# Attention backward: one block of E through GpSimd and the tile of G's products, and two more blocks of E turned by TensorE

## The chip, the cores and the metric

One Trainium2 chip, one of its cores. The core has five engines that run side by side and wait for each other by semaphores: TensorE (PE, with its weight loads as PEld), VectorE (DVE), ScalarE (ACT), GpSimd (POOL) and SyncE (SP, which here only issues DMAs). The metric is device time in microseconds; less is better. The kernel before takes 2192.32 us (median of 3 runs, 2185.16 to 2199.84).

## The reference

The kernel computes a transformer block and its gradients. With `x` of 2048 rows by 512, `xn = layernorm(x)`:

```python
out = x + attention(xn, wqkv, wo) * silu(mlp(layernorm(xn), w1, b1, w2, b2))
```

and the gradients of `out` against `x`, `wqkv`, `wo`, `w1`, `b1`, `w2` and `b2`. Attention has 32 heads of 16 columns each:

```python
scores = q @ k.T * Dh ** -0.5      # per head, 2048 x 2048
p = softmax(scores)
o = p @ v
```

Only attention's middle part concerns us. For each head and each tile of 128 keys by 512 queries the kernel forms E, the exponential of the scores, and G, which is E times (dO times V transposed). From E and G follow the output, the gradient of q (sums over keys) and, with E and G turned round so that queries lie on the partitions, the gradients of k and v (sums over queries).

## The kernel before

The work has three stages: a first one that prepares projections and hidden layers (until some 220 us), attention (220 to 1870 us), and the remaining gradients. The change lies in `attention_core`.

**Blocks and steps.** Attention runs over 64 blocks: 16 pairs of heads by 4 groups of 512 queries. A block has 16 steps, one per key block of 128 keys (`kb`). `g` counts the steps over all blocks, 1024 in all. The order of the work is written out by hand at the end of the function: one turn of the loop issues parts of several steps, so that the engines overlap. In the turn of step g, in program order:

- `emit_cO(g-2)`: a small DVE copy of one transposed 128x128 block from PSUM tile `tT` into `ek` (L1231), in some steps only.
- `emit_xt`, `emit_fin`: in steps 2 and 7, the end of the block before: a DVE copy (L1290), a reciprocal (L1310), and five small operations on GpSimd (L1311 to L1329), which also produce the weights W for Z.
- `emit_d(g)` and `emit_s(g+1)` on PE: two matmuls each, one per head of the pair. `s` has one PSUM buffer, `d` three.
- `emit_exp(g+1)`: ACT's exponential of `s` into `ets` (L1124).
- `emit_z(g-20)`: four matmuls on PE that sum up the gradients of k and v of the block before (L1350). Z is one PSUM buffer; eight units fill it (first the four for G, then the four for E), and DVE adds it to `acc` (L1364, or L1362 where it starts) in steps 3 and 11.
- `emit_x(g-1, ...)`: twelve matmuls on PE in three groups, for the sums over keys: two from E (L1248, L1251), one from G (L1255), which therefore waits for step g-1's products. The G group of step 0 is put off to step 2.
- `emit_T(g-1)`: PE turns blocks of E by matmul with the identity into `tT` (L1208, L1212), one PSUM buffer. In steps 1 and 6 `emit_XT` puts two more transposes, of float32, into the other half of `tT` (L1282).
- `emit_mult(g)`: two DVE products G = E x d, one per head, into `gts` (L1153). Between the two stand `xs`, a DVE copy in step 0 (L1264), and `acc`.
- In some steps a tick: a tiny GpSimd copy that reads `gts` (L1420) and holds back a load that GpSimd issues behind it.
- `emit_cT(g-1)`: ACT's copy of `tT` into `ek` (L1224).
- `emit_dmat(g)`: transposing DMAs that SP issues.

**How E and G are turned round.** A step's E has eight blocks of 128x128 (four query blocks, two heads), its G has eight too. G goes by DMA: after every second step one transposing DMA takes 16 blocks from `gts` (four buffers of two steps each) to `gk` (L1170). Of E's eight blocks PE turns seven, and the eighth goes by DMA from `ets` to `ekd` (L1180, L1184, L1186). `ets` is one tile of three slots of four steps each, used in turn, so that the exponential of step g writes where step g-12 stood. The eighth block is the last one (query block 3, second head) where `kb // 4` is even and the first one where it is odd, so that the two lie side by side in `ets` when two neighbouring slots are read; one DMA then takes eight blocks, every eight steps. Where the two slots are the last and the first of `ets`, there are two DMAs of four blocks.

**Which of the seven are put off.** In steps 1 and 6, where `tT` is shared, key blocks 0 and 5 have only four blocks turned at once (`cut` is 3). The other three of each go into later steps as an eighth transpose in `tT`, one per step, by the table `OLDER`: the key is the step whose transposes the block joins, the value is its key block and number. These are the blocks that the small DVE copy of `emit_cO` takes.

Of the kernel before, what the change touches and what calls it, by code (L numbers as in the profile page):

```python
# [1050 lines left out]
def attention_core(ctx, ctx_r, tc, k, grads, Oall, dQall, dKVT_out, ident_f32, ident_bf, npairs=16, nqc=4):  # L1051
# [12 lines left out]
    ekd = sb("ekd", 3)  # L1064
# [9 lines left out]
    ets = etp.tile([128, 3, 4, 2, 4, 128], bf16, name="ets")  # L1074
# [21 lines left out]
    def z_unit(g):  # L1096
        j = g // 16
        m = g % 8
        return (j, (g % 16) // 8, m % 4, m // 4) if 0 <= j < NB else None
# [4 lines left out]
    def emit_s(g, hj):  # L1104
        a = a_unit(g)
        if a is None:
            return
        j, kb = a
        op = op_of(j)
        qc = blocks[j][1]  # L1110
        r = 32 * hj
        if hj == 0:
            cur["s"] = ps_s.tile([128, 2, 512], f32, name="s")
        s = cur["s"]
        nc.tensor.matmul(s[:, hj, :], lhsT=op["KVT"][r:r + 32, kb * 128:(kb + 1) * 128], rhs=op["QDT"][r:r + 32, qc * 512:(qc + 1) * 512],  # L1115
                         start=True, stop=True, tile_position=(r, 0))
        st_et[g] = ets[:, g // 4 % 3]

    def emit_exp(g):

        a = a_unit(g)
        if a is None:
            return
        nc.scalar.activation(out=st_et[g][:, :, :, a[1] % 4, :].rearrange("k b h q -> k h b q"),  # L1124
                             in_=cur["s"][:].rearrange("k h (b q) -> k h b q", b=4), func=ACT.Exp)
# [15 lines left out]
    def emit_mult(g):  # L1141
        a = a_unit(g)
        if a is None:
            emit_xs(g - 1)
            emit_acc(g + ZOFF)
            return
        kb = a[1]
        if kb % 2 == 0:
            cur["gts"] = gtp.tile([128, 2, 2, 512], bf16, name="gts")
        gts = cur["gts"]  # L1150
        st_gt[g] = gts
        for hj in range(2):
            nc.vector.tensor_tensor(out=gts[:, kb % 2, hj, :].rearrange("k (b q) -> k b q", b=4),  # L1153
                                    in0=st_d.pop((g, hj))[:].rearrange("k (b q) -> k b q", b=4),
                                    in1=st_et[g][:, :, hj, kb % 4, :], op=ALU.mult)
            if hj == 0:
                emit_xs(g - 1)
                emit_acc(g + ZOFF)

    def emit_dmat(g):  # L1160
        a = a_unit(g)
        if a is None:
            return
        j, kb = a
        kc = kb // 4
        if kb % 4 == 1:
            blk[j]["Gk"][kc] = gbp.tile([128, 4, 2, 4, 128], bf16, name="gk")
        if kb % 2 == 1:
            gk = blk[j]["Gk"][kc][:, kb % 4 - 1:kb % 4 + 1]
            nc.sync.dma_start_transpose(out=gk.rearrange("q r h b k -> q (r h b) k"), in_=st_gt[g][:].rearrange("k a h q -> k (a h q)"))  # L1170


        sl = g // 4 % 3
        if kb % 8 == 4:
            ek = ekd.tile([128, 2, 4, 128], bf16, name="ekd")
            blk[j]["Ek"][(kc - 1, 3)] = ek[:, 0]
            blk[j]["Ek"][(kc, 3)] = ek[:, 1]
            blk[j]["ekd"] = ek
            if sl == 0:
                nc.sync.dma_start_transpose(out=ek[:, 0], in_=ets[:, 2, 3, 1].rearrange("k a q -> k (a q)"))  # L1180
        if kb % 8 == 6:
            ek = blk[j].pop("ekd")
            if sl == 0:
                nc.sync.dma_start_transpose(out=ek[:, 1], in_=ets[:, sl, 0, 0].rearrange("k a q -> k (a q)"))  # L1184
            else:
                nc.sync.dma_start_transpose(out=ek[:].rearrange("q c a k -> q (c a) k"),  # L1186
                                            in_=ets[:].rearrange("k s b h a q -> k (s b h) (a q)")[:, 8 * sl - 1:8 * sl + 1]
                                            .rearrange("k x q -> k (x q)"))
# [9 lines left out]
    def emit_T(g):  # L1198
# [7 lines left out]
        for i in range(cut(g), 7):  # L1206
            b = i + a[1] // 4 % 2
            nc.tensor.transpose(tb[:, i - cut(g), :], et[:, b // 2, b % 2, kk, :], ident_bf[:])  # L1208
        if older(g):
            kk2, i = older(g)  # L1210
            b = i + kk2 // 4 % 2
            nc.tensor.transpose(tb[:, 7, :], st_et[g // 16 * 16 + kk2][:, b // 2, b % 2, kk2 % 4, :], ident_bf[:])  # L1212
# [20 lines left out]
    def emit_x(g, part):  # L1233
# [9 lines left out]
        for c in range(4):  # L1243
            half, hj = c // 2, c % 2
            r = 32 * c
            ev = et[:, half::2, hj, kb % 4, :]
# [6 lines left out]
            else:  # L1253
                gv = st_gt[g][:, kb % 2, hj, :].rearrange("k (b q) -> k b q", b=4)[:, half::2, :]
# [77 lines left out]
    def emit_z(g):  # L1332
# [7 lines left out]
        for par in range(2):  # L1340
            kc = 2 * kp + par
            for hj in range(2):
                r = 64 * par + 32 * hj
                if part == 0:
                    mv = blk[j]["Gk"][kc][:, :, hj, qb, :]
# [4 lines left out]
                nc.tensor.matmul(Z[r:r + 32, :], lhsT=WT[j % 2][1 - part][:, qb, hj, :], rhs=mv,  # L1350
                                 start=(part == 0 and qb == 0), stop=(part == 1 and qb == 3), tile_position=(0, r))

    def emit_acc(g):
        u = z_unit(g)
        if u is None or u[2] != 3 or u[3] != 1:
            return
# [23 lines left out]
    for g in range(NSTEP - ZOFF):  # L1380
# [36 lines left out]
        for it in [x for x in late if x[0] <= g]:  # L1417
            late.remove(it)

            nc.gpsimd.tensor_copy(out=tick[:], in_=st_gt[g][0:1, kb % 2, 1, 510:512])  # L1420
# [123 lines left out]
```

## Time and profile before

| | |
|---|---|
| runs | 2192.32 us median, 2185.16 to 2199.84 |
| profiled execution | 2194.69 us, its span 2193.0 us, granted clock 0.995 |
| attention | some 220 to 1870 us of the span |
| PE, DVE, ACT, POOL busy, share of the span | 98%, 86%, 81%, 27% |
| exponentials (L1124) | 1024 of 1026 ns |
| ACT's copies of tT (L1224) | 898 of 532 ns (128x448), 126 of 372 ns (128x256) |
| products (L1153) | 2048 of 682 ns |
| small DVE copies (L1231) | 378 of 225 ns |
| transposes on PE (L1208, L1212) | 6790 and 378 |
| transposing DMAs gk<-gts | 512, 5.4 us from issue to landing (median) |
| transposing DMAs ekd<-ets | 171, 4.3 us from issue to landing (median) |

In a row of the profile stand the line of the kernel, the engine, the operation, the tile written and the tiles read, the shape, and the count; behind the bar the busy time in all, the mean duration of one in ns, and the idle time of the engine ahead of them with what ended it. Rows of a timeline start with the start in us from the span's beginning and the duration in us; several like instructions in a row are merged and counted (x3). Instructions of DVE, ACT and PE overlap at their ends: a product that takes 0.68 us lets the next one start after 0.60.

### The profile page before, as it was taken

The page shows a single profiled execution, that of the slowest core. Times are in us where ns is not written, and L with a number is a line of the kernel's source. Part 1 is how long each engine was busy: PE and PEld are TensorE (multiplying, and loading weights), DVE is VectorE, ACT ScalarE, POOL GpSimd, SP SyncE. Part 2 cuts the span into 40 slices and gives each one's busy share as a digit, 9 for nine tenths or more (in the row PEclk, how much of TensorE's full clock was granted, in tenths as well). Part 3 has the DMA queues.
Part 4 walks back from the last instruction along what each step waited for, and adds up shares of the span by engine and source line. Part 5 has one row for each costly group of instructions (what it writes and reads, how often), then busy time and mean ns, then how long its engine had stood idle before and what let it go on. Part 6 is the DMA issues. An engine that isn't in the chain of part 4 may idle for free.

```text
span 2193.0 us, 73789 instructions
## 1 busy us (share of the span) xinstructions
PE 2138.7 (98%) x30610; PEld 1173.8 (54%) x30659; DVE 1895.6 (86%) x3523; ACT 1782.5 (81%) x2481; POOL 596.8 (27%) x1373
## 2 busy tenths in 40 slices
PE   6999999999999999999999999999999999899999
PEld 3444555555555555555555555555555555444444
DVE  6677899999999999998999999999998998788647
ACT  5764899999999999998999999999998998675224
POOL 4275212232222222221313222222222222511003
PEclk9999999999999999999999999999999999999999
DMA  7786999999999999999999999999999999999975
GB/s 237 245 277 202 205 197 199 204 200 201 204 197 201 205 195 203 199 198 194 204 196 203 205 197 202 201 203 201 201 205 190 198 210 193 312 256 242 239 212 178
DMA packets 1422031, 461.11 MB, mean 210 GB/s; under 512 B 1334590, under 2 KB 1405886, under 8 KB 1421696
## 3 DMA queue, kind: packets, MB, share of 16 engines
q1 hardware_dynamic: 1407392, 425.46, 102.9%
q0 software_dynamic: 12720, 29.37, 5.1%
q8 instruction: 240, 3.93, 0.8%
q10 hardware_dynamic: 1584, 1.57, 0.2%
q14 instruction: 95, 0.78, 0.1%
HBM read 62.79 MB, written 64.75 MB: 58 GB/s over the span
## 4 chain that ended last, share of the span: by engine, by line
PE 89%; DMA 5%; DVE 3%; ACT 2%; issue 1%; SPq 1%; POOL 0%; DVEq 0%; ACTq 0%; POOLq 0%
PE tT L1208 21%; PE Z L1350 15%; PE d L1137 15%; PE X L1255 5%; PE X L1248 5%; PE X L1251 5%; PE s L1115 3%; DMA ekd<-ets 2%; PE ps_dy L909 2%; PE ps_dw L983 2%; PE ps_dw L742 2%; PE ps_h L352 2%; PE ps_m L367 2%; PE ps_dh L875 1%; PE ps_dxa L1027 1%; PE tT L1282 1%
## 5 line engine op out<-in xcount | busy, mean ns | idle before, releaser
L1153 DVE TENSOR_TENSOR gts<-d,ets 128x512 bf16<-128x512 f32 x2048 | 1302.1, 682 | 32.0 <-PE d L1137 13.7
L1124 ACT ACTIVATE ets<-s 128x1024 bf16<-128x1024 f32 x1024 | 1051.1, 1026 | 30.4 <-DMA ekd<-ets 10.3
L1224 ACT COPY ek<-tT 128x448 f32<-128x448 f32 (+1 forms) x1024 | 524.7, 512 | 114.9 <-PE tT L1208 33.2
L1208 PE MATMUL tT<-ident_bf,ets 128*128 128x128 bf16 x6790 | 558.4, 221 | 0.0
L1208 PEld LDWEIGHTS <-ets 128*128 128x128 bf16 x6790 | 382.8, 98 | 212.7 <-issue 199.7
L1137 PE MATMUL d<-QDT,KVT 32*128 32x512 bf16 x2048 | 478.4, 385 | 0.2 <-DVE gts L1153 0.2
L1115 PE MATMUL s<-QDT,KVT 32*128 32x512 bf16 x2048 | 401.9, 380 | 10.5 <-ACT ets L1124 10.4
L1248 PE MATMUL X<-ets,NAT 128*32 128x256 bf16 x4096 | 290.4, 273 | 0.0
L1251 PE MATMUL X<-ets,Lc 128*32 128x256 bf16 x4096 | 290.3, 273 | 0.0
L1255 PE MATMUL X<-gts,NAT 128*17 128x256 bf16 x4096 | 286.7, 273 | 0.0
L1350 PEld LDWEIGHTS <-W 128*32 128x32 bf16 x4096 | 105.7, 93 | 239.8 <-issue 236.9
L1420 POOL COPY tick<-gts 1x2 bf16<-1x2 bf16 x205 | 35.8, 174 | 728.6 <-DVE gts L1153 728.6
L1137 PEld LDWEIGHTS <-KVT 32*128 32x128 bf16 x2048 | 151.7, 90 | 114.5 <-issue 21.8
L1350 PE MATMUL Z<-gk,W 128*32 128x512 bf16 x2048 | 204.0, 390 | 1.4 <-DVE acc L1364 1.0
L1350 PE MATMUL Z<-ek,W 128*32 128x512 bf16 x1792 | 203.5, 389 | 0.0
L1251 PEld LDWEIGHTS <-Lc 128*32 128x32 bf16 x4096 | 109.9, 97 | 108.4 <-issue 0.5
L1231 DVE COPY ek<-tT 128x64 f32<-128x64 f32 x378 | 84.9, 225 | 90.9 <-ACT ek L1224 76.8
L1115 PEld LDWEIGHTS <-KVT 32*128 32x128 bf16 x2048 | 145.7, 91 | 25.5 <-issue 20.0
L1311 POOL TENSOR_TENSOR W<-NATQq,rL 128x128 bf16<-128x128 bf16 x64 | 25.5, 398 | 384.3 <-DVE rL L1310 328.7
L1255 PEld LDWEIGHTS <-NAT 128*17 128x17 bf16 x4096 | 112.9, 91 | 11.8 <-issue 3.1
L1248 PEld LDWEIGHTS <-NAT 128*32 128x32 bf16 x4096 | 109.5, 96 | 4.8 <-issue 4.7
L1350 PE MATMUL Z<-ekd,W 128*32 128x512 bf16 x256 | 99.6, 389 | 0.0
(252 smaller groups left out, 2467.2 us busy)
## 6 DMA issues: line engine op xcount, KB each, us to landing
gk<-gts SPq DMA_TRANSPOSE x512, 5.4
H1T_s<-h1r SPq DMA_DIRECT2D x28, 256.0 KB, 4.1
HGT_s<-hgT SPq DMA_DIRECT2D x8, 896.0 KB, 4.4
DH_s<-stg SPq DMA_DIRECT2D x12, 512.0 KB, 3.3
hch<-DH_s SPq DMA_DIRECT2D x12, 512.0 KB, 5.1
gp<-H1T_s SPq DMA_DIRECT2D x9, 512.0 KB, 7.1
out_dram<-ob_w POOLq DMA_DIRECT2D x36, 128.0 KB, 4.5
NAT_s<-NS SPq DMA_DIRECT2D x4, 1056.0 KB, 6.3
```

The source lines that it names most:

```text
L352: nc.tensor.matmul(ps[:], lhsT=w1_sb[:, ic, fc * 128:(fc + 1) * 128], rhs=yT[:, ic, g * 512:(g + 1) * 512], start=(ic == 0), stop=(ic == I ...
L1115: nc.tensor.matmul(s[:, hj, :], lhsT=op["KVT"][r:r + 32, kb * 128:(kb + 1) * 128], rhs=op["QDT"][r:r + 32, qc * 512:(qc + 1) * 512], start ...
L1124: nc.scalar.activation(out=st_et[g][:, :, :, a[1] % 4, :].rearrange("k b h q -> k h b q"), in_=cur["s"][:].rearrange("k h (b q) -> k h b q ...
L1137: nc.tensor.matmul(d[:], lhsT=op["KVT"][r:r + 32, kb * 128:(kb + 1) * 128], rhs=op["QDT"][r:r + 32, qc * 512:(qc + 1) * 512], start=True, ...
L1153: nc.vector.tensor_tensor(out=gts[:, kb % 2, hj, :].rearrange("k (b q) -> k b q", b=4), in0=st_d.pop((g, hj))[:].rearrange("k (b q) -> k b ...
L1208: nc.tensor.transpose(tb[:, i - cut(g), :], et[:, b // 2, b % 2, kk, :], ident_bf[:])
L1224: nc.scalar.copy(out=blk[j]["Ek"][kb // 4][:, kb % 4, c:7].rearrange("q i k -> q (i k)").bitcast(f32), in_=st_T[g][:, 0:(7 - c) * 64])
L1231: nc.vector.tensor_copy(out=blk[g // 16]["Ek"][kk // 4][:, kk % 4, i].bitcast(f32), in_=st_T[g][:, 448:512])
L1248: nc.tensor.matmul(X[r:r + 32, 0:256], lhsT=NATt[:, kb, hj, 1:33], rhs=ev, start=(kb == 0), stop=False, skip_group_check=True, tile_positi ...
L1251: nc.tensor.matmul(X[r:r + 32, 256:512], lhsT=Lc[:], rhs=ev, start=False, stop=False, skip_group_check=True, tile_position=(0, r))
L1255: nc.tensor.matmul(X[r:r + 17, 256:512], lhsT=NATt[:, kb, hj, 0:17], rhs=gv, start=False, stop=(kb == 15), skip_group_check=True, tile_pos ...
L1350: nc.tensor.matmul(Z[r:r + 32, :], lhsT=WT[j % 2][1 - part][:, qb, hj, :], rhs=mv, start=(part == 0 and qb == 0), stop=(part == 1 and qb = ...
```

## The change

Four things are altered together.

- E's eighth block no longer goes by a DMA of its own. In every step GpSimd copies it, 128x128, from `ets` into a ninth place of the `gts` tile, ahead of the products, and the DMA of `gts` takes 18 blocks in place of 16. `gk` has nine blocks per step, and Z reads the eighth block of E from there. `ekd` and its DMAs are gone.
- `ets` becomes 11 places of one step each, so that the exponential of step g writes where step g-11 stood, and a step's E lies together in memory. `gts` lists its blocks as eight and one.
- Key block 1 has only five blocks turned at once (`cut` is 2), and its other two join later steps: `OLDER` has eight entries in place of six. Before, the steps that take an older block are those with keys 4, 6, 7, 8, 12 and 13; after, 4, 6, 7, 8, 9, 10, 12 and 13.
- The four units of Z for E run from query block 3 down to 0, in place of 0 to 3, and `acc` follows the last one.

```diff
-    ekd = sb("ekd", 3)
...
-    ets = etp.tile([128, 3, 4, 2, 4, 128], bf16, name="ets")
+    NE = 11
+    ets = etp.tile([128, NE, 4, 2, 128], bf16, name="ets")
...
-        return (j, (g % 16) // 8, m % 4, m // 4) if 0 <= j < NB else None
+        return (j, (g % 16) // 8, m if m < 4 else 7 - m, m // 4) if 0 <= j < NB else None
...
-        st_et[g] = ets[:, g // 4 % 3]
+        st_et[g] = ets[:, g % NE]
...
-            cur["gts"] = gtp.tile([128, 2, 2, 512], bf16, name="gts")
+            cur["gts"] = gtp.tile([128, 2, 9, 128], bf16, name="gts")
...
+        b = 7 * (1 - kb // 4 % 2)
+        nc.gpsimd.tensor_copy(out=gts[:, kb % 2, 8, :], in_=st_et[g][:, b // 2, b % 2, :])
         for hj in range(2):
-            nc.vector.tensor_tensor(out=gts[:, kb % 2, hj, :].rearrange("k (b q) -> k b q", b=4),
+            nc.vector.tensor_tensor(out=gts[:, kb % 2, 4 * hj:4 * hj + 4, :],
...
-            blk[j]["Gk"][kc] = gbp.tile([128, 4, 2, 4, 128], bf16, name="gk")
+            blk[j]["Gk"][kc] = gbp.tile([128, 4, 9, 128], bf16, name="gk")
         if kb % 2 == 1:
             gk = blk[j]["Gk"][kc][:, kb % 4 - 1:kb % 4 + 1]
-            nc.sync.dma_start_transpose(out=gk.rearrange("q r h b k -> q (r h b) k"), in_=st_gt[g][:].rearrange("k a h q -> k (a h q)"))
...
-        sl = g // 4 % 3
-        if kb % 8 == 4:
-            ek = ekd.tile([128, 2, 4, 128], bf16, name="ekd")
...
-    OLDER = {4: (0, 0), 6: (0, 1), 7: (0, 2), 8: (5, 0), 12: (5, 1), 13: (5, 2)}
+            nc.sync.dma_start_transpose(out=gk.rearrange("q r x k -> q (r x) k"), in_=st_gt[g][:].rearrange("k a x q -> k (a x q)"))
+
+    OLDER = {4: (0, 0), 6: (0, 1), 7: (0, 2), 8: (1, 0), 9: (1, 1), 10: (5, 0), 12: (5, 1), 13: (5, 2)}
 
     def cut(g):
-        return 3 if g >= 16 and g % 16 in (0, 5) else 0
+        return {0: 3, 1: 2, 5: 3}.get(g % 16, 0) if g >= 16 else 0
...
                 elif 2 * qb + hj == 7 * (1 - par):
-                    mv = blk[j]["Ek"][(kc, 3)]
+                    mv = blk[j]["Gk"][kc][:, :, 8, :]
...
-        if u is None or u[2] != 3 or u[3] != 1:
+        if u is None or u[2] != 0 or u[3] != 1:
```

The other lines of the diff only follow the new shapes.

More of the change, by code (lines that the diff above doesn't have):

```diff
@@ L1207, in emit_T @@
             b = i + a[1] // 4 % 2
[L1208 removed]
+            nc.tensor.transpose(tb[:, i - cut(g), :], et[:, b // 2, b % 2, :], ident_bf[:])
         if older(g):
@@ L1245, in emit_x @@
             r = 32 * c
-            ev = et[:, half::2, hj, kb % 4, :]
+            ev = et[:, half::2, hj, :]
             if part == "e":
@@ L1350, in emit_z @@
                 nc.tensor.matmul(Z[r:r + 32, :], lhsT=WT[j % 2][1 - part][:, qb, hj, :], rhs=mv,
-                                 start=(part == 0 and qb == 0), stop=(part == 1 and qb == 3), tile_position=(0, r))
+                                 start=(part == 0 and qb == 0), stop=(part == 1 and qb == 0), tile_position=(0, r))
     def emit_acc(g):
         u = z_unit(g)
-        if u is None or u[2] != 3 or u[3] != 1:
+        if u is None or u[2] != 0 or u[3] != 1:
             return
@@ L1418, in attention_core @@
             late.remove(it)
-            nc.gpsimd.tensor_copy(out=tick[:], in_=st_gt[g][0:1, kb % 2, 1, 510:512])
+            nc.gpsimd.tensor_copy(out=tick[:], in_=st_gt[g][0:1, kb % 2, 7, 126:128])
             it[1]()
```

23 lines of the change are left out of this document (5 added, 18 removed).

## The prediction

> **What bounds the kernel now.** I read the page's first part, then the stage table, then one block of attention in the timeline. A "block" is 16 steps (one pair of heads, one fourth of the queries); a "step" is one key block. There are 64 blocks, and step n is the loop's turn with g mod 16 = n.
>
> ```profile
> PE 2138.7 (98%) x30610; PEld 1173.8 (54%) x30659; DVE 1895.6 (86%) x3523; ACT 1782.5 (81%) x2481; POOL 596.8 (27%) x1373
> ...
> 900.00:1200.00 300.00, 297.81 (x5102) 169.44 (x5102) 275.97 (x516) 272.92 (x375) 74.83 (x209) 0.99 1.19 199
> ```
>
> The second row is 300 us of attention: PE, DVE and ACT are busy for 298, 276 and 273 us. All three are nearly full, so any can set a step. Interval n is the time from exponential n's start to the next one's. A plain one takes 1.551 us, which is ACT's own sum (1.026 for the exponential, the rest for the copy of tT). Those behind an eighth transpose take 1.57 to 1.59. An undisturbed block takes 25.17 us (that of block 34, which begins at 1089.2).
>
> Stalls come on top, and the tile ekd shows the largest kind:
>
> ```profile
> L1186 SPq DMA_TRANSPOSE ekd<-ets x85: 1260/1270/2438, 234.0 to 1843.8; - x85
> ...
>   ACT ets L1124: 10.3, 11
> ```
>
> The second line is from "who waited for it": 11 exponentials sat idle for 10.3 us in all, until the transposing DMA had read the slot of ets that they write. One such place, PE's rows (the bracket is the idle time before) and the stretches around it (the column before the last two is the granted clock):
>
> ```profile
> 1029.79 0.38 PE L1137 MATMUL d<-QDT,KVT 32*128 32x512 bf16 x1
> 1031.97 0.39 PE L1115 MATMUL s<-QDT,KVT 32*128 32x512 bf16 x2 [1.80 <-ACT ets L1124]
> ...
> 1034.14 0.60 PE L1115 MATMUL s<-QDT,KVT 32*128 32x512 bf16 x2
> ```
> ```profile
> 1030.00:1032.00 2.00, 0.20 (x4) 0.02 (x2) 0.62 (x2) 1.10 (x2) 0.00 (x0) 1.00 0.98 218
> 1032.00:1034.00 2.00, 2.00 (x26) 1.14 (x25) 1.24 (x2) 1.37 (x2) 0.00 (x0) 0.64 1.19 269
> 1034.00:1036.00 2.00, 2.00 (x24) 0.69 (x23) 1.15 (x2) 1.56 (x2) 0.00 (x0) 0.51 1.10 234
> ```
>
> PE idles 1.80 us, and then its clock is 0.64 and 0.51 for 4 us. This stall costs 2.1 us at once and 1.4 after.
>
> **The change, part by part.**
>
> *1. The ekd transposes go: -15 us.* From block 1 on, the blocks exceed the undisturbed length by 22.9 us in total. Of that, 4.7 us recur with every change of the pair (0.23 us in its first block, 0.08 in its last) and stay. Of the 18.2 left, some 3 are single steps longer by 0.28 us at no fixed place; 15 stand in intervals 3 and 11, where exponentials 4 and 12 reuse the slot that SP's lagging ekd transfer still reads, and in the slow-clock steps behind them. Afterwards the slot of step g is written again at g+11, and its readers (PE, the products, GpSimd's copy) are then done for several us. Bounds: -18, and 0 if another late transfer takes the place.
>
> The clock is where a rule can be weighed. The row shows 1.80 us of idle followed by a clock of 0.64 and 0.51. The Trainium skill, "TensorE: Matmul & The Clock Gate" (section "Why this matters for your kernels"), asks for no idle gaps over about 3 us; by it no slow clock would follow here, and this part would be worth 12 rather than 15. The trace disagrees with it, and I go by the trace.
>
> *2. Key block 1 gives two blocks away: 0.* Step 2 carries the postponed products of key block 0 as well (eight X matmuls on L1255), and interval 3 behind it is 1.646 us. Two transposes fewer save 2 x 0.055 us there, and ACT's copy shrinks from 0.53 us towards the 0.37 of the 256-wide form. But the gain does not last: from step 0 to step 4 DVE runs without a gap (xs 0.68, two mults per step at a pitch of 0.60, xt 0.42, rL 0.20, acc 0.68). In block 34 the last X matmul of step 4 is already held until mult(3,1) ends (1097.39; the matmul starts at 1097.44, some 0.1 us late). PE coming 0.11 earlier waits 0.11 longer there. Bounds: -7 (63 x 0.11) and 0.
>
> *3. Two more small DVE copies, in steps 11 and 12: +22 us.* Before, the eighth transposes are issued in steps 5, 7, 8, 9, 13, 14, and the DVE copies two steps after their key block: 6, 8, 9, 10, 14, 15. After, steps 10 and 11 get an eighth transpose, and steps 11 and 12 a copy. Step 11 is one of the two that also add Z to acc. DVE in steps 10 to 12 of block 34:
>
> ```profile
> 1106.68 0.23 DVE L1231 COPY ek<-tT 128x64 f32<-128x64 f32 x1 [0.15 <-ACT ek L1224]
> 1106.82 1.89 DVE L1153 TENSOR_TENSOR gts<-d,ets 128x512 bf16<-128x512 f32 x3
> 1108.63 0.68 DVE L1364 TENSOR_TENSOR acc<-Z,acc 128x512 f32<-128x512 f32 x1
> 1109.23 1.88 DVE L1153 TENSOR_TENSOR gts<-d,ets 128x512 bf16<-128x512 f32 x3
> ```
> ```profile
> 1107.63 0.53 ACT L1224 COPY ek<-tT 128x448 f32<-128x448 f32 x1
> ...
> 1109.84 0.28 PE L1251 MATMUL X<-ets,Lc 128*32 128x256 bf16 x4
> 1109.95 0.30 PE L1255 MATMUL X<-gts,NAT 128*17 128x256 bf16 x4
> ```
>
> The small copy waits each time for ACT's copy of the same tT (bracket; all six kinds start 0.03 us behind ACT's end, and the next mult 0.17 behind it). In step 11 today, mult(11,0) starts at 1108.02, acc at 1108.63, mult(11,1) at 1109.23 and ends at 1109.91; the X matmul of step 12 that needs it starts at 1109.95, 0.11 behind the group before it, which is PE's own pitch. The slack is nil. After: the eighth transpose moves ACT's copy to about 1107.69, it ends at 1108.21, the small copy follows, and mult(11,0) starts at 1108.38: 0.36 late. acc, mult(11,1) and the X matmul follow, Z of step 12 waits for acc, the transposes of step 12 come 0.35 late, and so do s and the exponential of the next step, which today start as soon as ACT is free. 63 blocks x 0.35 = 22 us. Queued behind the added wait on DVE are mult(11,0), acc and mult(11,1); PE waits for the last. Nothing returns it: later steps are set by ACT at 1.551, and DVE is idle again (0.48) before step 14. Bounds: 63 x 0.14 (the copy's own pitch, without the wait) = 9, and 63 x 0.37 = 23. I take the long value because all six existing kinds show the wait. The two steps with eight transposes cost at most 63 x 2 x 0.02 = 3 beside it, and nothing where step 11's chain is longer.
>
> *4. 1024 copies on GpSimd: 0.* No row has a 128x128 copy there. The nearest:
>
> ```profile
> L1420 POOL COPY tick<-gts 1x2 bf16<-1x2 bf16 x205 | 35.8, 174 | 728.6 <-DVE gts L1153 728.6
> L223 POOL COPY NS<-nat 128x512 bf16<-128x512 bf16 x32 | 19.4, 633 | 43.3 <-ACT nat L215 42.1 <-DVE nat L217 1.1
> ```
>
> A straight line between the means (174 and 633 ns) gives 0.29 us for 128 elements; the ends are 0.17 and 0.63. 16 x 0.29 = 4.6 us per block on top of the 6.3 (75 of 300) leaves GpSimd under half busy. Each copy stands ahead of its step's tick and behind the five small operations of steps 2 and 7. Step 7 is the tight one: in block 34 these run from 1102.63 to 1104.62, behind a tick and a load, so copy(7) ends near 1104.9, while mult(7,1), which alone released the transfer, ended at 1103.44. The transfer thus gets ready 1.5 us later. Its tile of gts is wanted again by step 14 (its mult starts at 1113.1): 8.2 us later, against 5.4 us median and 8.6 at most from issue to landing. So it is covered, nearly always; without that cover each late microsecond would hold DVE, and PE behind it.
>
> *5. SP: 0.* Per eight steps it transposes 4 x 16 + 8 = 72 blocks of 128x128 today in five or six instructions, and 4 x 18 = 72 afterwards in four. An ekd issue takes 1.2 to 1.3 us of SP even for four blocks, a gk issue 1.6 at least (median 2.3, its wait counted), so SP is relieved; the rate per block is the open point (below). Z's second half runs in the other order with as many matmuls, and what it reads has landed some ten steps earlier.
>
> **Sum.** -15 + 0 + 22 + 0 + 0 = +7 us. The profiled execution took 2194.69 (span 2193.0 and 1.7 around it), so it would take 2202; the median of the runs shown is 2192.32, 2.4 lower, so the forecast is 2199. About 1% (22 us) is what a measurement of this kernel can tell from no change.
>
> **Rivals.**
>
> *The step-11 chain is shorter than I think.* If the new copies don't wait for ACT, or DVE finds slack for them, part 3 is at most 9, and part 2 may pay some of its 7: -15 - 3 + 4 = -14, so 2178 (2172 to 2188). For it: DVE is idle 0.15 us before step 10's copy and 0.48 before step 14's. Against: neither idle time lies between step 11's start and its acc.
>
> *The lag lives on.* The exponential no longer waits for ekd, but the 18-block transfer of a late step 7 or 15 does not free gts in time, and DVE stalls where ACT did; part 1 is then 0 and the sum +22: 2214 (2207 to 2222). For it: the largest landing time (8.6) is over the 8.2 that I count. Against: DVE waited only 0.6 us in all for gk transfers, though SP lagged then too.
>
> *The transposes bind (the slower side).* Place: SP's queue. In block 31 SP issued without a pause from 1010.45 to 1034.70: 140 blocks in 24.25 us, 5.77 per us; the kernel asks for 72 in 12.58, 5.72 per us. The point from which it decides is a rate 1% lower. If rows of 18 blocks go at 5.5, eight steps take 13.1 us, 0.5 more, 127 times: +64, about 2263 with the small terms. Against: the DMA packets are 256 bytes each whatever the row's length, and fewer instructions should raise the rate.
>
> *The port.* The small copies, xs and xt are DVE copies, and some will meet a GpSimd copy. If that locks them out for 0.29 us, the four or so per block with no slack behind them (steps 0 to 4, 11 and 12) would cost 63 x 4 x 0.29 = 73: 2272. In the rows, the 63 small copies that lie beside GpSimd's two-input operations take 225 ns, as the others do, and the 425 mults that do take 681, as the others do. The Trainium skill, "SBUF — State Buffer" (section "Who interferes with whom"), says that copies can enter a mode that takes a port pair shared with GpSimd, and that the loser is then held for the whole instruction. By that rule this rival would be the outcome; the trace does not bear it out for sources in PSUM, which all of these copies have.
>
> **How the numbers follow.** The forecast (2190 to 2206) gets 0.55, the shorter chain 0.21, the lag 0.12, the transposes 0.06, the port 0.03, and 0.03 is left for a faster surprise. The ends of the terms give -18 - 7 + 9 = -16 and 0 + 0 + 26 = +26, so 2176 to 2218 without the two dear rivals, which leaves out some 0.15; that is the range. Faster by over 1% (under 2170.4): 0.04. Slower by over 1% (over 2214.2): half of the lag's and both dear rivals, 0.14. Within 1%: 0.82.
>
> **What would show it.** Part 1: no exponential waits for a DMA, no stretch of attention with a clock under 0.9. Part 2: interval 3 falls from 1.65 to about 1.55, and interval 5 rises by as much. Part 3: interval 13 (exponential 13 to 14) grows from 1.55 to about 1.90, the X matmul of step 12 starts right behind mult(11,1), and step 11's small copy shows idle time behind ACT's copy. Part 4: GpSimd's copies at 0.29, mults still at 681 ns. Part 5: landing no later than about 6 us. The prediction is wrong if step 11's mult starts on time, if DVE waits for gk or GpSimd, or if mults get longer.

## The result and the profile after

The changed kernel took 2199.85 us (median of 22 runs, 2194.92 to 2217.09), the kernel before in the same comparison 2193.21 (22 runs, 2185.16 to 2203.54). The ratio is 1.0031, 95% interval 1.0017 to 1.0045. On another chip (the last experiment below) it was 1.0012, 0.9997 to 1.0026. So the change costs some 3 to 7 us; the first comparison tells this from nothing, the second does not. The forecast was 2199. The profiled execution took 2199.02 us, its span 2197.3.

The same two rows as before, the busy time of the whole span and 300 us of attention (PE, PEld, DVE, ACT, POOL, then granted clock, DMA share and GB/s):

```profile
PE 2149.0 (98%) x30659; PEld 1177.0 (54%) x30659; DVE 1916.6 (87%) x3649; ACT 1780.1 (81%) x2481; POOL 869.3 (40%) x2397
```
```profile
900.00:1200.00 300.00, 298.37 (x5108) 169.77 (x5109) 280.34 (x541) 272.79 (x376) 125.58 (x400) 1.00 1.13 200
```

DVE went from 276 to 280 us in this stretch, where it has its two more small copies per block, and GpSimd from 75 to 126. PE and ACT look as they did. What costs the time shows only in the lengths of single steps. These are the medians of the sixteen intervals over blocks 1 to 62, in ns, taken from the starts of the exponentials in each trace. In the last three columns stand the sum of the sixteen, then the 62 blocks together in us, and what of that lies above 62 undisturbed blocks:

```
interval     0    1    2    3    4    5    6    7    8    9   10   11   12   13   14   15 |   sum  62 blocks  above
before    1554 1551 1552 1646 1558 1644 1558 1574 1570 1573 1577 1558 1552 1554 1589 1562 | 25172  1583.6  22.9
after     1556 1551 1553 1552 1666 1647 1556 1575 1570 1575 1575 1576 1574 1880 1556 1594 | 25556  1587.7   3.3
```

Two large effects nearly cancel. The time above the undisturbed block fell from 22.9 us to 3.3, and the undisturbed block grew by 0.384 us, 23.8 us over 62 blocks. Most of the growth is interval 13 (+326 ns). The difference is +4.1 us, as the profiled executions have it (2199.02 against 2194.69).

Of the first effect, the exponentials' group shows what is gone. The columns behind the last bar are idle time before the instruction and what ended it; before, the first entry of this row was the DMA of `ekd`, with 10.3 of 30.4 us:

```profile
L1124 ACT ACTIVATE ets<-s 128x1024 bf16<-128x1024 f32 x1024 | 1051.6, 1027 | 16.7 <-PE d L1137 3.9 <-issue 1.4 <-POOL ndr L1299 0.2
```

The second effect is for the most part one place in each block. This is the changed kernel's timeline in steps 11 and 12 of block 34 (start, duration, engine, line; the bracket is idle time before). First DVE:

```profile
1108.93 1.29 DVE L1155 TENSOR_TENSOR gts<-d,ets 128x512 bf16<-128x512 f32 x2
1110.33 0.22 DVE L1215 COPY ek<-tT 128x64 f32<-128x64 f32 x1
1110.47 0.68 DVE L1155 TENSOR_TENSOR gts<-d,ets 128x512 bf16<-128x512 f32 x1
1111.07 0.68 DVE L1348 TENSOR_TENSOR acc<-Z,acc 128x512 f32<-128x512 f32 x1
1111.67 0.68 DVE L1155 TENSOR_TENSOR gts<-d,ets 128x512 bf16<-128x512 f32 x1
```

Then ACT and PE in the same window:

```profile
1109.77 0.53 ACT L1208 COPY ek<-tT 128x448 f32<-128x448 f32 x1
...
1111.81 0.40 PE L1334 MATMUL Z<-gk,W 128*32 128x512 bf16 x4
...
1112.24 0.45 PE L1239 MATMUL X<-gts,NAT 128*17 128x256 bf16 x4
...
1112.41 0.09 PEld L1239 LDWEIGHTS <-NAT 128*17 128x17 bf16 x2 [0.17 <-issue]
1112.62 0.56 PE L1192 MATMUL tT<-ident_bf,ets 128*128 128x128 bf16 x7
```

ACT's copy of tT ends at 1110.30, the added small copy starts 0.03 behind it, mult(11,0) at 1110.47, the addition to `acc` at 1111.07, mult(11,1) at 1111.67, ending at 1112.35. Four Z matmuls start at 1111.81, when the addition has read Z. The four X matmuls that read the products take 0.45, where the prediction's row of the same place has 0.30: the first starts at 1112.24 and the other three only at 1112.40, just behind mult(11,1). The transposes and the next s follow 0.3 late.

### The profile page after: what moved, and what is told of

Same layout as the page of the kernel before. It is cut to its first block, busy times and chain, and to the rows that moved or that the text cites. A ratio compares the mean times of both kernels' runs of the same rounds, so it can differ in the third digit from the quotient of the medians.

```text
span 2197.3 us, 74997 instructions
## 1 busy us (share of the span) xinstructions
PE 2149.0 (98%) x30659; PEld 1177.0 (54%) x30659; DVE 1916.6 (87%) x3649; ACT 1780.1 (81%) x2481; POOL 869.3 (40%) x2397
## 4 chain that ended last, share of the span: by engine, by line
PE 87%; DVE 6%; ACT 3%; DMA 2%; SPq 1%; issue 1%; POOL 0%; DVEq 0%; ACTq 0%; POOLq 0%
PE tT L1192 20%; PE Z L1334 15%; PE d L1137 14%; PE X L1239 6%; PE X L1232 5%; PE X L1235 5%; PE s L1115 3%; PE ps_dw L983 2%; PE ps_dy L909 2%; PE ps_h L352 2%; PE ps_dw L742 2%; PE ps_m L367 2%; DVE gts L1155 2%; ACT ek L1208 2%; PE ps_dh L875 1%; DVE acc L1348 1%
## 5 line engine op out<-in xcount | busy, mean ns | idle before, releaser
L1208 ACT COPY ek<-tT 128x448 f32<-128x448 f32 (+2 forms) x1024 | 518.4, 506 | 135.0 <-PE tT L1192 57.0
L1192 PE MATMUL tT<-ident_bf,ets 128*128 128x128 bf16 x6664 | 550.9, 221 | 0.0
L1192 PEld LDWEIGHTS <-ets 128*128 128x128 bf16 x6664 | 375.4, 98 | 210.5 <-issue 195.2
L1137 PE MATMUL d<-QDT,KVT 32*128 32x512 bf16 x2048 | 467.4, 384 | 0.0
L1153 POOL COPY gts<-ets 128x128 bf16<-128x128 bf16 x1024 | 280.3, 297 | 389.5 <-ACT ets L1124 388.1
L1334 PE MATMUL Z<-gk,W 128*32 128x512 bf16 x2304 | 302.9, 389 | 9.7 <-DVE acc L1348 1.1
L1239 PE MATMUL X<-gts,NAT 128*17 128x256 bf16 x4096 | 300.2, 273 | 0.0
L1137 PEld LDWEIGHTS <-KVT 32*128 32x128 bf16 x2048 | 145.9, 91 | 114.3 <-issue 21.5
L1215 DVE COPY ek<-tT 128x64 f32<-128x64 f32 x504 | 112.6, 223 | 97.1 <-ACT ek L1208 76.1
L1115 PEld LDWEIGHTS <-KVT 32*128 32x128 bf16 x2048 | 139.6, 91 | 12.2 <-issue 6.8
L1196 PE MATMUL tT<-ident_bf,ets 128*128 128x128 bf16 x504 | 110.4, 219 | 0.0
```

The costliest lines, as they stand in the source:

```text
L1137: nc.tensor.matmul(d[:], lhsT=op["KVT"][r:r + 32, kb * 128:(kb + 1) * 128], rhs=op["QDT"][r:r + 32, qc * 512:(qc + 1) * 512], start=True, ...
L1153: nc.gpsimd.tensor_copy(out=gts[:, kb % 2, 8, :], in_=st_et[g][:, b // 2, b % 2, :])
L1208: nc.scalar.copy(out=blk[j]["Ek"][kb // 4][:, kb % 4, c:7].rearrange("q i k -> q (i k)").bitcast(f32), in_=st_T[g][:, 0:(7 - c) * 64])
L1215: nc.vector.tensor_copy(out=blk[g // 16]["Ek"][kk // 4][:, kk % 4, i].bitcast(f32), in_=st_T[g][:, 448:512])
L1239: nc.tensor.matmul(X[r:r + 17, 256:512], lhsT=NATt[:, kb, hj, 0:17], rhs=gv, start=False, stop=(kb == 15), skip_group_check=True, tile_pos ...
```

## The experiments

Times of a run are compared with runs of the kernel before on the same chip; a ratio is to these, with its 95% interval.

### 1. Each half alone

The change without its second part:

```diff
-    OLDER = {4: (0, 0), 6: (0, 1), 7: (0, 2), 8: (1, 0), 9: (1, 1), 10: (5, 0), 12: (5, 1), 13: (5, 2)}
+    OLDER = {4: (0, 0), 6: (0, 1), 7: (0, 2), 8: (5, 0), 12: (5, 1), 13: (5, 2)}
...
-        return {0: 3, 1: 2, 5: 3}.get(g % 16, 0) if g >= 16 else 0
+        return 3 if g >= 16 and g % 16 in (0, 5) else 0
```

> The change without its second part: the GpSimd copy and the 18-block transposes stay, the blocks of E are given away in the steps of the kernel before (six of them, none of key block 1). Theory (the transposes of E by DMA cost 15 to 20 us, the two more small copies on DVE gave 22 to 24 back, the copies on GpSimd cost nothing): the excess over the undisturbed block falls from 22.9 us to about 3, the intervals 11 to 15 stand as before (1558, 1552, 1554, 1589, 1562 ns), so about 20 us under the kernel before, some 2174 us, ratio 0.991; by the prediction's own term of 15 us it would be 2177. Rival (the copies on GpSimd or the longer transposes have a price of their own, which the saved transposes covered): between 2185 and 2200 us, with multiplications longer than the 682 ns of before or stalls left on gk. Rival of the clock gate (12 us): 2181 us.

Measured: 2181.13 us against 2196.99, ratio 0.9926 (0.9915 to 0.9938), so -16 us. The 62 blocks take 1568.9 us, 14.8 less than before; the part above the undisturbed block is 5.2 (before 22.9), and the undisturbed block is 25.220 (25.172). The products take 683 ns. The theory holds in the main, nearer to the prediction's own 15 than to the 20 that I had made of it after the result. The 20 was missed twice over: the part above the undisturbed block did not fall to 3, and the undisturbed block did not stand as before. It is 0.048 us longer (intervals 4, 13 and 15 have 1574, 1588 and 1593 ns, interval 14 fell to 1557), 3.0 us over 62 blocks. So the GpSimd copies, the 18-block transposes and the new order show this price together; which of them it belongs to is not shown. The 2181 us of the rival with the clock was met only as a number: the kernel before stood at 2196.99 on this chip, and 12 us less would have been 2185. This version is faster than both kernels.

The second part alone, on the kernel before (the same two edits the other way round):

> The kernel before, with only the second part of the change: two blocks of E of key block 1 transposed in the steps of key blocks 8 and 9, and two of key block 5 moved to 10 and 12. The transposes of E by DMA stay, GpSimd copies nothing. Theory (the small copies in steps 11 and 12 alone make the loss): interval 13 goes from 1554 to about 1880 ns, 11 and 12 rise by some 20 each, the intervals 3 and 4 change places, so 22 to 24 us over the kernel before, about 2216 us, ratio 1.010 to 1.011. Rival (the loss needs the GpSimd copies beside it, or the tile of 18 blocks): less than 5 us over the kernel before, interval 13 below 1650 ns. Rival (the longer steps give the transposes of E by DMA time to land): 2200 to 2208 us, with interval 13 at 1880 and the stalls of 18 us at half.

Measured: 2208.63 us, ratio 1.0057 (1.0042 to 1.0073), +12.5 us (9 to 16). Interval 13 has the median 1876, 11 and 12 have 1575 and 1576, 3 fell to 1551 and 4 rose to 1641. So the undisturbed block grows as the theory says, by 0.355 us or 22 us in all, and needs neither the GpSimd copy nor the new tile for it. But the time rose by little more than half of that. The stalls were not halved, as the third reading had it: 21.3 us stand above the undisturbed block, before 22.9, and the wait for the DMA is all there.

```profile
L1124 ACT ACTIVATE ets<-s 128x1024 bf16<-128x1024 f32 x1024 | 1051.1, 1027 | 38.4 <-DMA ekd<-ets 13.4 <-PE d L1137 4.4 <-ACT ek L1224 2.9
```

A part of the answer stands in the single blocks. In 13 of 62, interval 13 is under 1700 ns, and these are blocks with a stall in interval 11 just ahead (1785 to 2816 ns), in which DVE has caught up before its copy is late. There the two losses are not added, which is worth some 13 x 0.3 = 4 us. But the profiled execution of this kernel was the longest of its six (2216.2), and its 62 blocks take 20.4 us more than those of before, with these 4 us already saved. What made the median 7.6 us shorter than this execution is in no trace and stays open. The halves measured alone add up to -4 us, the whole to +3 to +7, so they are not quite independent.

### 2. Which of the two added copies

Only the copy in step 11 is left (seven blocks given away, one of them of key block 1):

```diff
-... 8: (1, 0), 9: (1, 1), 10: (5, 0), 12: (5, 1), 13: (5, 2)}
+... 8: (1, 0), 9: (5, 0), 12: (5, 1), 13: (5, 2)}
...
-        return {0: 3, 1: 2, 5: 3}.get(g % 16, 0) if g >= 16 else 0
+        return {0: 3, 1: 1, 5: 3}.get(g % 16, 0) if g >= 16 else 0
```

> The changed kernel with seven blocks given away in place of eight: the step of key block 10 gets none, key block 1 gives one block away and not two. So of the two added small copies of DVE only that of step 11, beside the addition of Z, is left. Theory (this copy alone makes the loss): interval 13 stays near 1880 ns, above 1800 in any case, and the time near that of the changed kernel, 2196 to 2203 us. Rival (the loss is the sum of both copies, half each): interval 13 near 1720 ns, some 10 us less than the changed kernel, 2187 to 2192 us.

Only the copy in step 12 (the same, with `10: (5, 0)` in place of `9: (5, 0)`):

> The counterpart: seven blocks, the step of key block 9 gets none, so that of the two added small copies only that of step 12 is left. Theory (the copy in step 11 makes the loss): interval 13 falls to 1580 to 1650 ns (a copy in step 13 was worth 57 ns there), and the time to that of the change without its second part or up to 4 us more, 2181 to 2186 us on the chip of the first four runs, ratio 0.992 to 0.995. Rival (half each): interval 13 near 1720 ns, 2187 to 2192 us, ratio 0.996 to 0.998.

All transposes stay, but DVE's copy in step 11 is left out:

```diff
         kk, i = older(g)
+        if g % 16 == 9:
+            nc.gpsimd.memset(blk[g // 16]["Ek"][kk // 4][:, kk % 4, i], 0.0)
+            return
         nc.vector.tensor_copy(
```

> The changed kernel, all its transposes in place, without the small copy of DVE in step 11: the block is transposed into the tile tT but never read from there, GpSimd writes zeros in its place in the tile of E, so one block of key block 5 or 1 is zero in the output's sums (part of the computation is left out). Theory (the copy on DVE is the cost, not the eighth transpose on PE): interval 13 falls from 1878 to 1580 to 1650 ns, 14 to 18 us come back, 2182 to 2187 us. Rival (the eighth transpose on PE is the cost): interval 13 stays above 1800 ns, 2195 to 2203 us.

Measured on one chip (the kernel before 2193.04), with the medians of three intervals and the block:

```
                           time      ratio (95%)                interval 12   13   14    block
copy in step 11 only     2200.44   1.0024 (1.0005 to 1.0044)           1559 1897 1558    25568
copy in step 12 only     2182.66   0.9928 (0.9905 to 0.9951)           1594 1559 1594    25258
step 11's copy off DVE   2181.65   0.9928 (0.9904 to 0.9952)           1576 1571 1579    25251
```

All three fall as the theory has it, within a microsecond and some 20 ns of the bounds that it gave. The copy in step 11 alone makes the whole loss, the one in step 12 nothing that can be measured, and the eighth transpose on PE is not the cost, for it stays in the third kernel. DVE in the same steps of block 34 with only the copy in step 12:

```profile
1099.61 1.89 DVE L1155 TENSOR_TENSOR gts<-d,ets 128x512 bf16<-128x512 f32 x3
1101.41 0.68 DVE L1348 TENSOR_TENSOR acc<-Z,acc 128x512 f32<-128x512 f32 x1
1102.01 0.68 DVE L1155 TENSOR_TENSOR gts<-d,ets 128x512 bf16<-128x512 f32 x1
1102.61 0.21 DVE L1215 COPY ek<-tT 128x64 f32<-128x64 f32 x1
```

Exponential 12 starts at 1100.85 here and at 1110.20 in the changed kernel. Counted from there, the addition starts at 0.56 and mult(11,1) at 1.16; with the copy in step 11 it is 0.87 and 1.47. So the copy, 0.22 long, makes both late by 0.31, since it has to wait for ACT first. The second kernel also still gives one block of key block 1 away, and is no faster than the one that gives none (0.9928 and 0.9926): giving it away gains nothing that shows.

### 3. Other places for the copy

The eight blocks in other steps, none with its copy beside the addition:

```diff
-    OLDER = {4: (0, 0), 6: (0, 1), 7: (0, 2), 8: (1, 0), 9: (1, 1), 10: (5, 0), 12: (5, 1), 13: (5, 2)}
+    OLDER = {3: (0, 0), 4: (0, 1), 6: (0, 2), 7: (1, 0), 8: (1, 1), 11: (5, 0), 12: (5, 1), 13: (5, 2)}
```

> The changed kernel, with the same eight blocks given away in the steps of key blocks 3, 4, 6, 7, 8, 11, 12, 13 in place of 4, 6, 7, 8, 9, 10, 12, 13: the small copies of DVE stand in steps 5 and 13 in place of 11 and 12, none beside the addition of Z. Theory (the copy in the step of the addition is the price): interval 13 falls from 1878 to under 1600 ns, 18 us or more come back; the copy in step 5 stands behind the five steps in which DVE is late, and can cost up to its 0.29 us there (0 to 18 us over 62 blocks), so 2176 to 2194 us, the middle of which, 2182, is the likeliest. Rival (eight small copies on DVE cost this wherever they stand): 2197 to 2203 us, with the lost time in another interval.

Measured: 2186.02 us, ratio 0.9953 (0.9940 to 0.9965). Interval 13 has 1645, intervals 4 and 5 have 1670 and 1703, the block 25.336. So 0.22 of the 0.384 us came back. Interval 13 did not fall under 1600, as the theory had it. Against the kernel without the second part (25.220), the copy in step 5 costs 57 ns in the intervals 3 to 5 together, and the one in step 13 as much in interval 13. A small copy of DVE costs between nothing and 0.31 us here, by its step.

The copy of step 11 moved behind both multiplications:

```diff
-        emit_cO(g - 2)
+        if g % 16 != 11:
+            emit_cO(g - 2)
...
         emit_mult(g)
+        if g % 16 == 11:
+            emit_cO(g - 2)
```

> The changed kernel, with one operation moved: in step 11 the small copy of DVE stands behind both multiplications and the addition, not ahead of them. Theory (the copy ahead of them makes mult(11,0), the addition and mult(11,1) late, and the matmuls of G and Z in step 12 wait for these): interval 13 falls from 1878 to about 1600 ns, some 18 us come back, 2180 us. Rival (DVE has no slack for this copy anywhere between steps 11 and 13): the loss moves to interval 14 or stays, 2195 to 2203 us. Rival (the tile tT that is held longer stops the transposes of step 12): PE waits ahead of them for DVE, 2190 to 2205 us.

Measured: 2278.6 us, ratio 1.0378 (1.0364 to 1.0391), some 80 us slower than the changed kernel. The third reading named the mechanism and was far off in its price. There is one buffer for tT, so the transposes of step 11 wait until the small copy has read it. PE's rows in block 34:

```profile
1149.79 0.28 PE L1239 MATMUL X<-gts,NAT 128*17 128x256 bf16 x4
1151.55 0.55 PE L1192 MATMUL tT<-ident_bf,ets 128*128 128x128 bf16 x7 [1.47 <-DVE ek L1215]
```

PE stands for 1.47 us in each block (63 times, 92.8 us in all); interval 12 becomes 3102 ns, and interval 13 is back at 1557, because DVE catches up meanwhile. The run says that the copy cannot go there, and nothing on whether DVE has room for it.

### 4. What GpSimd's copies cost

The copy done twice:

```diff
-        nc.gpsimd.tensor_copy(out=gts[:, kb % 2, 8, :], in_=st_et[g][:, b // 2, b % 2, :])
+        for _ in range(2):
+            nc.gpsimd.tensor_copy(out=gts[:, kb % 2, 8, :], in_=st_et[g][:, b // 2, b % 2, :])
```

> The changed kernel, with the copy on GpSimd done twice in each of the 1024 steps: 1024 more copies of 0.297 us, 304 us more of GpSimd's time. Theory (the copy lies in GpSimd's idle time and takes nothing from DVE): the time of the changed kernel within 4 us, 2196 to 2204 us, the multiplication at 681 to 684 ns, gk landing as before. Rival (GpSimd's copy holds up DVE's access to the memory): each copy beside a multiplication lengthens it; at the prediction's price of 0.07 us a copy the multiplications rise by 35 ns on average and the time by up to 70 us.

Measured: 2252.8 us, ratio 1.0259 (1.0217 to 1.0301), 53 us above the changed kernel. Nearly every interval is 1640 ns. By the time alone the rival had won. But the row that it named did not move: the products take 683 ns, and the small copies 224. What moved is the start of the exponential. ACT's rows in the doubled kernel, and then in the changed one:

```profile
1118.80 0.53 ACT L1209 COPY ek<-tT 128x448 f32<-128x448 f32 x1
1119.42 1.02 ACT L1124 ACTIVATE ets<-s 128x1024 bf16<-128x1024 f32 x1
...
1121.06 1.02 ACT L1124 ACTIVATE ets<-s 128x1024 bf16<-128x1024 f32 x1
```
```profile
1109.77 0.53 ACT L1208 COPY ek<-tT 128x448 f32<-128x448 f32 x1
...
1110.20 1.03 ACT L1124 ACTIVATE ets<-s 128x1024 bf16<-128x1024 f32 x1
...
1111.77 1.03 ACT L1124 ACTIVATE ets<-s 128x1024 bf16<-128x1024 f32 x1
```

From the start of the copy to that of the exponential it is 0.62 us in place of 0.43. The instruction lists of the three kernels say what differs, the engines for which most exponentials wait:

```
before        exponential waits for DVE, PE, ACT
changed       exponential waits for DVE, PE, POOL
copy twice    exponential waits for PE, DVE, ACT, POOL
```

With three, the trace shows one separate wait instruction ahead of the exponential, which holds the waits for DVE and PE. With four it shows two, one for PE and a second behind it for two others (38 ns, starting 55 ns after the first started), and the exponential starts 0.17 us behind the end of s in place of 0.09.

The number of waits alone does not explain it, for the kernel before has a counter-example. In 169 of its 1024 exponentials, a DMA of `ekd` comes to the three engines as a fourth, and two wait instructions stand ahead. These are the rows of the wait instructions (ACTq) on the exponential's line, before and with the copy done twice:

```profile
L1124 ACTq EVENT_SEMAPHORE  x1183: 17/358/1456, 219.8 to 1853.8; - x198
...
L1124 ACTq EVENT_SEMAPHORE  x2028: 17/38/38, 217.6 to 1909.5; - x185
```

Of the exponentials 8 of blocks 1 to 62 in the kernel before, 21 have two wait instructions and 41 have one. Both kinds start 0.11 us behind the end of s and 1574 ns behind the exponential ahead of them (medians). The difference is in the order. There the first instruction waits for DVE alone (17 ns in block 34), and PE's wait stands in the second, with the DMA's. In the doubled kernel the first waits for PE, and the second starts only when s has ended.

To test the wait apart from the memory, GpSimd got other work that leaves the exponential's waits as they are:

```diff
-    outp.tile([128, 96], mybir.dt.uint8, name="pad_to_256c")
+    scr = outp.tile([128, 48], bf16, name="scr")
...
         nc.gpsimd.tensor_copy(out=gts[:, kb % 2, 8, :], in_=st_et[g][:, b // 2, b % 2, :])
+        for i in range(2):
+            nc.gpsimd.tensor_copy(out=scr[:], in_=ident_bf[:, 48 * i:48 * i + 48])
```

> The changed kernel, with GpSimd's own copy as it stands and, behind it in each of the 1024 steps, two copies of 128x48 of the identity into a tile that nobody reads; the exponential waits for the same three engines as in the changed kernel, where the kernel with the copy done twice made it wait for a fourth, ACT itself. Theory (the 53 us of the copy done twice came from the added wait of the exponential, not from the memory): the time of the changed kernel within 4 us, 2196 to 2204 us, steps of 1551 to 1580 ns as before, the multiplication at 681 to 684 ns. Rival (more work on GpSimd holds up DVE or ACT through the memory): steps near 1640 ns and 2230 to 2260 us, as with the copy done twice.

The changed kernel beside it, on the same chip:

> The changed kernel as it is, on the same chip as the kernel with the scratch copies. Every theory expects 2196 to 2204 us, ratio 1.002 to 1.005, and interval 13 near 1880 ns; it is the other side of the comparison.

Measured: 2202.64 us with the scratch copies (ratio 1.0027, 1.0006 to 1.0047), 2199.41 without (1.0012, 0.9997 to 1.0026). The block is 25.560 and 25.554 us, interval 13 is 1878 in both. The page of the kernel with the scratch copies:

```profile
L1157 DVE TENSOR_TENSOR gts<-d,ets 128x512 bf16<-128x512 f32 x2048 | 1308.5, 683 | 11.4 <-PE d L1137 3.7
...
L1155 POOL COPY scr<-ident_bf 128x48 bf16<-128x48 bf16 x2048 | 457.1, 223 | 63.1
```

The scratch copies take 457 us of GpSimd, where the doubled copy added 303, and the time differs by 3 us, with intervals that overlap. So more work of GpSimd beside DVE and ACT is not what the doubled copy cost. That it was a second wait instruction behind PE's is what the traces and this run leave; it was not tried by adding or moving a wait alone.

## Why the prediction was right

**The sum, +7.** Right, with some luck. In the traces the part above the undisturbed block fell by 19.6 us and the undisturbed blocks grew by 23.8, where -15 and +22 were forecast; the two misses have opposite signs. That the median came out within 1 us of 2199 is chance as well: the two comparisons put the change at +6.6 and +3.2 us. One addition is off: half of the lag's chance and both dear rivals make 0.15 for slower by over 1%, not 0.14.

**What sets a plain step.** The prediction has 1.551 us as "ACT's own sum", the exponential and the copy of tT. That reading is wrong. In the step with the short copy of `tT` the interval is as long (1552 ns), and ACT stands idle for 0.12 us between the copy and the exponential. These are ACT's rows from exponential 2 to exponential 3 of block 34 in the kernel before, then PE's s between them:

```profile
1092.30 1.02 ACT L1124 ACTIVATE ets<-s 128x1024 bf16<-128x1024 f32 x1
1093.36 0.37 ACT L1224 COPY ek<-tT 128x256 f32<-128x256 f32 x1
1093.85 1.02 ACT L1124 ACTIVATE ets<-s 128x1024 bf16<-128x1024 f32 x1
...
1093.38 0.39 PE L1115 MATMUL s<-QDT,KVT 32*128 32x512 bf16 x2
```

`s` has one buffer, so s starts 0.06 us behind the exponential that read it, takes 0.38, and the next exponential starts 0.09 behind its end: 1.024 + 0.06 + 0.38 + 0.09 = 1.55. No faster copy would shorten such a step. With 0.17 in place of 0.09 the same loop gives 1.64, the step of the kernel with the copy done twice. The forecast did not suffer by it, since its terms rest on measured intervals.

**1. The ekd transposes, -15.** Right in size: -16 us measured alone (ratio 0.9926), -14.8 in the blocks of the trace. But that kernel also has the GpSimd copies and the 18-block transposes, and its -14.8 is a sum: 17.7 us of stalls went, nearly all of the 18.2 that the prediction had beside what stays, and 3.0 came back in the undisturbed block. Only the first exponential of the changed kernel has a DMA among its waits, and the granted clock is 1.00 from 228 to 1860 us. By the time alone, 12 us lie outside the interval of 13.6 to 18.7; but as two effects are mixed in it, the clock is better read from the rows of the kernel before, in which it fell to 0.51 and 0.50 behind two gaps of under 2 us.

**2. Key block 1 gives two blocks away, 0.** Right in the sum (intervals 3 and 4 together have 3204 ns before and 3218 after), wrong in the place. Interval 3 fell by 94 ns as forecast, but interval 4 rose by 108, not interval 5. The step that failed is "the last X matmul of step 4 is already held until mult(3,1) ends": it is held so still, but PE stands already one step earlier, where the matmul d of step 3 waits for mult(2,0) to free its buffer (in block 34 that product ends at 1097.08, and the matmul starts at 1097.13).

**3. The copies in steps 11 and 12, +22.** Right, and the chain is as it was told: the wait for ACT, mult(11,0), the addition, mult(11,1), the X matmuls of step 12. Interval 13 became 1.880 (forecast about 1.90). Counted from exponential 12, the addition and mult(11,1) are 0.34 later than in the kernel before (there 0.53 and 1.13 behind its start at 1108.10), where 0.36 was forecast. Against the version without the second part the block is 0.336 us longer, 20.8 us, and the time differs by 0.0086 of 2197, 19 us (by the first comparison's ratio, 23). The wait for ACT was the uncertain part, and its long value was the true one. On the kernel before the same edit costs only 12.5; a stall of `ekd` hides it in 13 blocks there, and the rest of the difference is open. The prediction added the parts as if each stood alone.

**4. GpSimd's copies, 0.** Right, but for what they may have of the 3.0 us of part 1. The estimate of 0.29 us each was 0.297 in the profile, the products take 682 ns, and more GpSimd work changes nothing that can be told. These are the rows of the changed kernel's page:

```profile
L1155 DVE TENSOR_TENSOR gts<-d,ets 128x512 bf16<-128x512 f32 x2048 | 1308.0, 682 | 11.5 <-PE d L1137 2.6
...
L1153 POOL COPY gts<-ets 128x128 bf16<-128x128 bf16 x1024 | 280.3, 297 | 389.5 <-ACT ets L1124 388.1
```

What the prediction left out is that the copy puts GpSimd among those for whom the exponential waits. It took the place of ACT in that list, so the wait for PE stayed in the last wait instruction; in the kernel with the copy done twice it did not, and that kernel is 53 us slower.

**5. SP and the 18-block transposes, 0.** Right, but for the same 3.0 us. The transposes of the changed kernel, issue times (minimum, median, maximum in ns) and times to landing:

```profile
L1172 SPq DMA_TRANSPOSE gk<-gts x512: 1810/2544/4994, 227.7 to 1861.1; - x171
...
DMA to landing us min/median/max: 3.8/5.5/7.7
```

The sign "no later than about 6 us" holds for the median, 5.5, not for the latest, 7.7; that is still under the 8.2 that I counted as the room in the tight step, and nobody waits for a DMA out of `gts`.

**The rivals.** The shorter chain failed on interval 13. The lag did not live on (5.2 us above the undisturbed block in the first experiment, and 3.3 in the changed kernel). The transposes did not bind: they would have cost 0.5 us per eight steps, and the undisturbed block of the first experiment is 0.05 us longer than before. The port is refuted for these copies: the small copies take 223 to 225 ns and the products 682 to 683 with GpSimd busy 27, 40 and 57% of the span, and the 112 small copies of the changed kernel that lie beside a GpSimd copy take 225 ns. What the Trainium skill says in "SBUF — State Buffer" (section "Who interferes with whom"), that a copy in a mode with the shared port pair and GpSimd hold each other up for a whole instruction, no row here shows; these copies read PSUM. The same section lets a copy into such a mode only when its operands meet certain conditions. The prediction's sentence that by that rule this rival would be the outcome leaves the conditions out and makes the rule wider than it is.

## What to carry to other kernels

A small operation costs what it does to the chain behind it, not its length: the same 0.22 us copy was worth 0, 0.06 or 0.31 us per block by the step in which it stood. Before work is moved, look for the step in which its engine already carries something extra, and keep it out of there; here the first part of the change alone, with the old places, is the fastest whole version (2181.13 us, ratio 0.9926), level with the one that has only the copy in step 12. Before an engine is made faster, check that it is what sets the step: in the plain steps here it was the loop through the one buffer of `s`. And when an engine is given a new reader or writer of a shared tile, look at the waits of the instruction on the critical path and at their order, not only at the work added.

## What the runs showed of the hardware that I had not expected

**A wait instruction behind the wait that ends last** goes with some 0.09 us per step: 1640 ns in nearly every interval of the kernel with the copy done twice, where plain ones had 1551 to 1558. Two wait instructions in the other order, in 169 exponentials of the kernel before, go with no such loss.

**The clock after an idle PE.** Where PE stood still 1.45 to 1.49 us in each of 63 gaps of the kernel with the copy behind the multiplications, the clock stayed at 1.00. These are 2-us stretches of it, the first two of which hold the gap:

```profile
1149.00:1151.00 2.00, 1.07 (x21) 0.55 (x21) 2.00 (x4) 1.46 (x2) 0.62 (x3) 1.00 1.15 271
1151.00:1153.00 2.00, 1.45 (x28) 0.86 (x27) 0.74 (x4) 0.81 (x2) 0.00 (x0) 1.00 1.31 252
1153.00:1155.00 2.00, 2.00 (x41) 1.23 (x34) 2.00 (x4) 1.98 (x3) 0.38 (x2) 1.00 1.27 287
```

In the kernel before, a gap of 1.86 us that ends at 1683.0 is followed by this:

```profile
1683.00:1685.00 2.00, 2.00 (x30) 1.00 (x29) 1.29 (x2) 1.81 (x3) 0.15 (x1) 0.88 1.26 294
1685.00:1687.00 2.00, 2.00 (x27) 1.16 (x24) 1.29 (x2) 1.14 (x2) 0.00 (x0) 0.50 1.15 230
1687.00:1689.00 2.00, 2.00 (x30) 0.89 (x27) 1.08 (x3) 1.54 (x2) 0.00 (x0) 0.77 1.05 239
```

The clock fell in the same way behind the gap of 1.80 in the prediction, and behind one of 2.18 in the second part alone (0.52, then 0.63). Two of 1.24 us, one in each of these two kernels, were followed by 1.00. One of 1.36 us, early in attention in the second part alone, was followed by 0.50, though the 63 longer ones were not. So the length of the gap alone does not decide here.
